# Spectral and attention layers on one core: three row blocks of the second spectral layer prepared inside the first attention loop

## The chip, the cores and the metric

The kernel runs on one core of a Trainium2 chip. A core has five engines that work side by side, each through its own instructions in order: TensorE (PE; its weight loads are listed as PEld), VectorE (DVE), ScalarE (ACT), GpSimd (POOL) and SyncE (SP, which here only starts transfers). They share an on-chip memory, and PE writes its results to a second one, PSUM, of eight banks. The metric is the time of one execution on the device in microseconds; lower is better.

## The reference

Two pairs of layers work on x, a bf16 array of 2048 rows by 512. A spectral layer normalises each row, takes a real 2-D Fourier transform, multiplies with fixed complex weights, transforms back and adds the result to x. An attention layer normalises each row, makes queries of 32 heads of 16 numbers, and one set of keys and values for all heads, and adds the projected result to x.

```
def _A_ref(x, w_r, w_i):
    X = rfft2(x.astype(float32), axes=(-2, -1))
    X = X * (w_r + 1j * w_i)
    return irfft2(X, s=(S, D), axes=(-2, -1)).astype(bfloat16)

def _B_ref(x, wq, wk, wv, wo):
    q = (x @ wq).reshape(B, S, 32, 16).transpose(0, 2, 1, 3)
    k, v = x @ wk, x @ wv
    scores = einsum("bhqd,bkd->bhqk", q, k) * 16 ** -0.5
    p = softmax(scores, axis=-1)
    o = einsum("bhqk,bkd->bhqd", p, v)
    return o.transpose(0, 2, 1, 3).reshape(B, S, 512) @ wo

x = x + _A_ref(_layernorm(x), A_w_r, A_w_i)
x = x + _B_ref(_layernorm(x), B_wq, B_wk, B_wv, B_wo)
x = x + _A_ref(_layernorm(x), A_w_r, A_w_i)
x = x + _B_ref(_layernorm(x), B_wq, B_wk, B_wv, B_wo)
```

## The kernel before, in words

Everything stays on the chip between the layers. The 2048 rows lie as `x_sb[p, r, t, :]`: 128 partitions p, four row groups r (each 512 rows), four interleaved parts t. A row block t is the four groups r at one t. The outer loop (`pair`) runs twice: a spectral layer, then an attention layer.

**Spectral layer.** For each row block t, `scaled` normalises the four groups (`Norm.apply`: one ACT or DVE instruction of 128x512 for each group, from the row statistics that `Norm.stats` made on DVE and that `Norm.root` and `Norm.scales` turned into a factor and an offset). `butterfly` (L155) then takes sums and differences of the four groups and of the halves of their columns: six DVE `tensor_tensor` operations, which write Z, block t. Z lies in the buffer `xz`, which holds the transposed rows `xT` for the queries and keys during attention. `odd_sums` and `even_sums` are PE matmuls with Z as the stationary operand and a table of cosines and sines as the moving one: a length-2048 transform cut to a quarter by the butterfly. A group of odd sums adds over all four row blocks in one PSUM bank, so its last matmuls need block 3. `middle` then transforms over the width, multiplies with the weights and transforms back over the width; `blocks` transforms back over the rows with the tables IO and IE, adds to x, and makes `xT`, the keys and the values of the attention layer.

The front differs between the two spectral layers. `front_first` waits for loads. `front_next` (L863), the second layer's, follows the first attention loop: block 3 of x (and only it) is still without its attention result, since the last query block's last head group has just ended. It scales blocks 0 to 2, and between their butterflies and sums it finishes that last projection: `last_scale` divides by the softmax sums and transposes back (DVE), `last_project` multiplies with wo (PE, three of four pieces ahead of `last_scale`, the fourth behind it), `last_residual` adds to x (DVE). Then statistics, root and scaling of block 3, its butterfly, its sums.

**Attention loop** (`Attention.run`). It has 32 groups, eight for each query block (512 queries), a group being four heads. A group has 64 tiles of 128 keys by 512 queries for one head. The loop goes in some 579 steps, about 18 in a group; a step's work on each engine is put in an order by hand, and `chain` (L422) fixes that order for PE, ACT, DVE and Pool. In a step
- PE makes scores for two or three tiles (`act_step`) and ACT takes their exponential in one instruction (L609);
- 19 tiles of a group get no exponential from ACT. For them DVE turns scores into a bf16 bit pattern (`dv_pass`, L643, `t_new`); three shifted copies of that pattern ("images") are added up instead of an exact exponential. DVE makes two of the images for a whole phase at once (`image_step`, L658, `s_new`, at the first and the fourth of a phase's six steps) and Pool the third tile by tile (L662, `pool_new`);
- PE multiplies exponentials and images with the values (`pv_step`, L622), two or more steps later.

`pace` (L535) makes a Pool instruction wait for the newest s_new, so Pool works in bursts between two of them. Other work comes at fixed steps: `evict` takes a group's result (DVE transpose, L550), `normalise` divides it (Pool, L565, `od_new`), `turned_back` transposes (DVE, L571), `piece` makes the next group's queries or projects a row group of the query block before (PE), and `residual` (L587) adds it to x on DVE. Some steps later, as `STAT` says, `finish` calls `row_done`: in the first loop the row's statistics (DVE) and, when a block's four rows are done, four small Pool instructions for its factors and offsets; in the second loop the store of the row to HBM, from SP or Pool in turn. `later` and `later_pool` queue such work on DVE and Pool.

Behind the second loop the last projection is made with four PSUM banks (pool `psE`), DVE adds, and the last four rows are stored.

Outside the loops a scheduler may move an instruction ahead, but within each manual schedule the order of PE, ACT and DVE is the program's. PSUM and work memory are handed from one stage's pools to the next tile by tile.

## Time and profile before

| what | us |
|---|---|
| median of 3 runs | 1586.08 (1585.1 to 1587.77) |
| the profiled execution's own time | 1586.75 |
| its span on the core | 1584.6 |
| busy ACT / DVE / PE / POOL | 1445.6 / 1418.6 / 1363.6 / 795.8 |
| L609, exponentials | 1315.7 in 1158 |
| L643, t_new on DVE | 792.3 in 1204 |
| L662, pool_new on Pool | 747.1 in 1204 |
| L658, s_new on DVE | 385.9 in 380 |

The span is what the profiler saw on the core; the time has some 2 us more around it. Busy time is what an engine's instructions took. In lists of groups, instructions of one source line, engine and shape stand together. In a timeline a row is a start, a duration, the engine, the line, what is written and read, how many equal instructions follow each other, and in brackets how long the engine had been idle and what released it. In the chain, the work that ended last is followed back, at each step to what released it. The granted clock is the share of TensorE's full clock.

### The profile page before, as it was taken

Reading aid. Unit: us, or ns where it says so; the run is one execution under the profiler, and the core shown is the slowest. Engines: PE = TensorE matmul, PEld = TensorE weight load, DVE = VectorE, ACT = ScalarE, POOL = GpSimd, SP = SyncE. Lnnn points to the kernel's source line nnn. Section 1 sums busy time; section 2 is a strip of 40 time slices with the busy share of each in tenths; the row PEclk is TensorE's granted clock in tenths of the full one; section 3 lists DMA queues with packets and bytes.
Section 4 is the critical chain, followed back from the end, with each engine's and each line's share of the span. In section 5 each row is a group of like instructions: output and inputs, shape, how many; then the busy total and the mean of one; then the engine's idle time right before and its main releaser. Section 6 shows DMA issues by size and latency. Waiting matters only on the chain.

```text
span 1584.6 us, 33064 instructions
## 1 busy us (share of the span) xinstructions
PE 1363.6 (86%) x13244; PEld 430.9 (27%) x13244; DVE 1418.6 (90%) x2260; ACT 1445.6 (91%) x1358; POOL 795.8 (50%) x1310
## 2 busy tenths in 40 slices
PE   5978888899889988898879688888998899889987
PEld 2432222222222222222234322222222222222222
DVE  6587999999999999999866889999999999999996
ACT  6658999999999999999944599999999999999997
POOL 1003655565656565656600045555556656665555
PEclk9997999999999999999989789999999999999999
DMA  7000000000000000000000000000000000000000
GB/s 269 14 1 1 2 1 1 1 1 2 1 2 1 2 1 1 1 2 1 2 0 1 1 1 2 1 2 1 5 5 5 5 5 5 5 5 5 5 1 21
DMA packets 12910, 15.37 MB, mean 10 GB/s; under 512 B 5716, under 2 KB 10452, under 8 KB 12628
## 3 DMA queue, kind: packets, MB, share of 16 engines
q1 hardware_dynamic: 12372, 12.22, 2.3%
q8 instruction: 103, 1.69, 0.5%
q0 software_dynamic: 384, 1.05, 0.2%
q14 instruction: 51, 0.42, 0.1%
HBM read 11.17 MB, written 2.10 MB: 8 GB/s over the span
## 4 chain that ended last, share of the span: by engine, by line
DVE 36%; ACT 31%; PE 15%; issue 14%; POOL 4%; DMA 0%; DVEq 0%; POOLq 0%; ACTq 0%
ACT e L609 30%; DVE t_new L643 16%; DVE s_new L658 9%; POOL pool_new L662 4%; PE pv_new L622 3%; PE sc L531 3%; PE new L199 3%; DVE st L103 2%; PE new L286 2%; DVE o L550 1%; DVE qt L345 1%; DVE ot_new L571 1%; PE dv L531 1%; PE new L235 1%; PE new L234 1%
## 5 line engine op out<-in xcount | busy, mean ns | idle before, releaser
L609 ACT ACTIVATE e<-sc 128x1536 bf16<-128x1536 f32 (+1 forms) x1158 | 1315.7, 1293 | 21.9 <-PE dv L531 19.3
L662 POOL TENSOR_SCALAR pool_new<-t_new 128x512 int16<-128x512 int16 x1204 | 747.1, 643 | 746.7 <-DVE s_new L658 566.4
L643 DVE TENSOR_SCALAR t_new<-dv 128x512 uint16<-128x512 f32 x1204 | 792.3, 678 | 77.1 <-PE dv L531 62.3
L622 PE MATMUL pv_new<-e,vaug 128*32 128x512 bf16 x2892 | 593.3, 388 | 0.0
L531 PE MATMUL sc<-qt,KT 32*128 32x512 bf16 x2892 | 457.8, 386 | 117.0 <-ACT e L609 109.9
L531 PE MATMUL dv<-qt,KT 32*128 32x512 bf16 x1204 | 455.1, 387 | 21.5 <-DVE t_new L643 19.7
L622 PE MATMUL pv_new<-s_new,vaug 128*32 128x512 bf16 x2408 | 421.1, 385 | 5.7 <-DVE s_new L658 5.7
L658 DVE TENSOR_SCALAR s_new<-t_new 128x3584 int16<-128x3584 int16 (+1 forms) x380 | 385.9, 1016 | 0.1
L622 PE MATMUL pv_new<-pool_new,vaug 128*32 128x512 bf16 x1204 | 298.7, 386 | 21.1 <-POOL pool_new L662 21.1
L531 PEld LDWEIGHTS <-KT 32*128 32x128 bf16 x4096 | 155.9, 91 | 561.6 <-issue 555.2
L622 PEld LDWEIGHTS <-vaug 128*32 128x32 bf16 x7708 | 153.8, 94 | 397.6 <-issue 365.4
L622 PE MATMUL pv_new<-t_new,vaug 128*32 128x512 bf16 x1204 | 232.0, 386 | 0.1
L340 PE MATMUL ps<-xz,wq_sb 128*128 128x512 bf16 x256 | 67.2, 385 | 0.6 <-ACT KT L386 0.6
L199 PE MATMUL new<-tab_F,xz 128*128 128x512 bf16 x192 | 52.7, 433 | 9.9 <-DVE xz L164 9.9
L550 DVE STREAM_TRANSPOSE o<-pv_new 128x512 f32<-128x512 f32 x64 | 45.3, 707 | 13.6 <-PE pv_new L622 13.6
L103 DVE BATCH_NORM_STATS2 st<-x_sb 128x6 f32<-128x512 bf16 x64 | 43.0, 671 | 3.8 <-DMA x_sb<-in_A_x_dram 3.5
L345 DVE CAST qt<-ps 128x512 bf16<-128x512 f32 x64 | 43.6, 682 | 1.2 <-PE ps L340 1.2
L565 POOL TENSOR_TENSOR od_new<-o,den 128x256 bf16<-128x256 f32 x62 | 38.5, 620 | 0.0
L107 ACT ACTIVATE ln_rstd<-ln_mv,ln_eps 128x4 f32<-128x4 f32 x13 | 3.9, 297 | 29.6 <-DVE ln_mv L104 29.4
L340 PEld LDWEIGHTS <-wq_sb 128*128 128x128 bf16 x256 | 21.9, 97 | 31.1 <-issue 16.3
L199 PEld LDWEIGHTS <-xz 128*128 128x128 bf16 x192 | 20.2, 109 | 36.5 <-DVE xz L164 11.2
L318 PE MATMUL new<-G_new,tab_IE 128*128 128x512 bf16 x128 | 28.9, 379 | 0.0
(92 smaller groups left out, 614.0 us busy)
## 6 DMA issues: line engine op xcount, KB each, us to landing
tab_F<-const_F SPq DMA_DIRECT2D x4, 640.0 KB, 11.9
x_sb<-in_A_x_dram SPq DMA_DIRECT2D x4, 512.0 KB, 4.6
rt<-in_A_w_r_dram SPq DMA_DIRECT2D x1, 1028.0 KB, 7.5
rt<-in_A_w_i_dram SPq DMA_DIRECT2D x1, 1028.0 KB, 11.7
tab_IE<-const_IE SPq DMA_DIRECT2D x1, 1024.0 KB
out_dram<-x_sb SPq DMA_DIRECT2D x8, 128.0 KB, 1.7
out_dram<-x_sb POOLq DMA_DIRECT2D x8, 128.0 KB, 2.2
tab_I<-const_I SPq DMA_DIRECT2D x1, 768.0 KB, 6.0
```

Source lines behind the costliest of these rows:

```text
L103: self.nc.vector.bn_stats(st, x_ap)
L199: self.mm(ps, lhsT=z, rhs=tab, start=(t == 0 and (i == 0 or mms[i - 1][1] != 0)), stop=(t == T - 1 and i == len(mms) - 1))
L340: self.nc.tensor.matmul(ps, lhsT=self.aw["wq"][:, c, hg, :], rhs=self.xT[:, c, 4 * qb:4 * qb + 4, :].rearrange("d k p -> d (k p)"), start= ...
L345: self.nc.vector.tensor_copy(out=qt, in_=ps)
L531: nc.tensor.matmul(dst, lhsT=KT[hs, kc * P:(kc + 1) * P], rhs=QT[g][hs, :], start=True, stop=True)
L550: nc.vector.transpose(out=o.rearrange("p c j -> p (c j)"), in_=ps)
L565: return engine.tensor_tensor(out=turned_od[g // 2][:, :, half], in0=o[:, :, 0:DH], in1=den.unsqueeze(2).broadcast_to([P, 16, DH]), op=ALU ...
L609: nc.scalar.activation(out=e[:, 0:na, :], in_=sc[:, 0:na, :], func=ACT.Exp, scale=SCALE)
L622: nc.tensor.matmul(pv[g][32 * h:32 * h + 32, :], lhsT=vaug[:, max(j, 0), kc, :], rhs=rhs, start=(first_pv[(g, h)] == u), stop=(last_pv[(g, ...
L643: nc.vector.tensor_scalar(out=tb[(g, b)][:, i, :], in0=dv, scalar1=T_MUL, scalar2=T_ADD, op0=ALU.mult, op1=ALU.add)
L658: image[0] = nc.vector.tensor_scalar(out=s_new[:, lo:nt, :], in0=src[:, lo:nt, :], scalar1=PH_OFF[i], scalar2=None, op0=ALU.add)
L662: pace(nc.gpsimd.tensor_scalar(out=sb[(g, b, 3)][:, i, :], in0=src[:, i, :], scalar1=1.0, scalar2=PH_OFF[3], op0=ALU.mult, op1=ALU.add))
```

## The change

Row blocks 0 to 2 of the second spectral layer are scaled and go through their butterfly inside the first attention loop. When the fourth row of a block has its statistics, `finish` queues, behind the four small Pool instructions, four scalings on Pool (every second step), and then the butterfly: for blocks 0 and 1 on Pool, cut into 20 pieces of 256 elements a partition, one every second step; for block 2 on DVE in six whole operations at fixed steps of the last group. The results go to Z, whose blocks now lie in `xz` as `(i t)` and not `(t i)`: block t of Z fills exactly the place of query block t's transposed rows, which are free by then. For block 2's four rows the steps at which their statistics are taken (in the second loop: their stores) move ahead by up to two groups.

`front_next` is left with the last projection, block 3 and the sums: all sums of blocks 0 to 2 follow each other. The last projection no longer ends with an add on DVE: PE multiplies the old rows with an identity matrix into the same PSUM bank ahead of the projection, and ACT (behind the second loop ACT and DVE in turn) copies the sum to x. Its four banks come from the stage's own pool. Block 3 is scaled by one ACT and three DVE instructions.

For the space of the new tiles the tables IO and IE are no longer kept all the time: they lie in each spectral layer's work pool, and are loaded twice.

```diff
+LAST_B = (13, 14, 16, 16, 17, 18)
...
+def butterfly_pieces(nc, engine, norm, small, x_sb, Z, t, width):
+    tiles = {}
+    tt = engine.tensor_tensor
+    def scaled(r):
+        if r == 0:
+            X_new = small.tile([P, 4, 512], BF, tag="bx", bufs=1)
+            s_new = small.tile([P, 2, 512], BF, tag="bs", bufs=1)
+            e_new = small.tile([P, 4, 512], BF, tag="be", bufs=1)
+            tiles.update(X=X_new, s=s_new, e=e_new)
+        norm.apply(nc.gpsimd, x_sb[:, r, t, :], tiles["X"][:, r, :], r, t)
+    def first(op, a, b):
+        X, dst = tiles["X"], tiles["s"] if op is ALU.add else tiles["e"][:, 2:4, :]
+        return tt(out=dst[:, :, a:b], in0=X[:, 0:2, a:b], in1=X[:, 2:4, a:b], op=op)
+    def second(op, a, b):
+        sm = tiles["s"]
+        return tt(out=tiles["e"][:, 0 if op is ALU.add else 1, a:b], in0=sm[:, 0, a:b], in1=sm[:, 1, a:b], op=op)
+    def third(op, a, b):
+        e, lo = tiles["e"], 0 if op is ALU.add else 256
+        return tt(out=Z[:, t, :, lo + a:lo + b], in0=e[:, :, a:b], in1=e[:, :, 256 + a:256 + b], op=op)
+    rows = [lambda r=r: scaled(r) for r in range(R)]
+    rest = []
+    for fn, n, w in ((first, 512, width // 2), (second, 512, width), (third, 256, width // 4)):
+        for op in (ALU.add, ALU.subtract):
+            rest += [lambda fn=fn, op=op, a=a, w=w, n=n: fn(op, a, min(a + w, n)) for a in range(0, n, w)]
+    return rows, rest
...
-            g, i = divmod(k, 4)
-            g = min(HG * (g + 1) + 5 + i, NG - 1)
-            later(max(2, s0[g] + STAT - now[0]), lambda: finish(k))
-
-        def finish(k):
-            for i, fn in enumerate(row_done(k % 4, k // 4) or ()):
+            if t == NQB - 2:
+                n = s0[NG - 3 + r // 2] + (4, 14)[r % 2]
+            else:
+                n = s0[HG * (t + 1) + 5 + r] + STAT
+            later(max(2, n - now[0]), lambda: finish(r, t))
+
+        def finish(r, t):
+            roots = row_done(r, t) or ()
+            for i, fn in enumerate(roots):
                 later_pool(1 + i, fn)
+            if roots:
+                own = t == NQB - 2
+                rows, rest = butterfly_pieces(nc, nc.vector if own else nc.gpsimd, self.norm, small, x_sb, self.Z, t, 2048 if own else 256)
+                for i, fn in enumerate(rows):
+                    later_pool(len(roots) + 2 + 2 * i, lambda fn=fn: fn())
+                for i, fn in enumerate(rest):
+                    if own:
+                        later(s0[NG - 1] + LAST_B[i] - now[0], fn)
+                    else:
+                        later_pool(len(roots) + 10 + 2 * i, lambda fn=fn: pace(fn()))
...
+        def last_project(i, ps, end):
+            ot = otc[NQB - 1]
             if not end:
-                ps_new = psum.tile([P, 512], F32, tag="mm", bufs=bufs)
-                last_ps[i] = ps_new
+                nc.tensor.matmul(ps, lhsT=tabs["EYE"][:, 0, :], rhs=x_sb[:, i, T - 1, :], start=True, stop=False)
             for c in (3,) if end else range(3):
-                nc.tensor.matmul(last_ps[i], lhsT=otc[NQB - 1][:, c, i * P:(i + 1) * P], rhs=wo_sb[:, c, :], start=(c == 0), stop=(c == 3))
-
-        def last_residual(i):
-            nc.vector.tensor_tensor(out=x_sb[:, i, T - 1, :], in0=last_ps.pop(i), in1=x_sb[:, i, T - 1, :], op=ALU.add)
+                nc.tensor.matmul(ps, lhsT=ot[:, c, i * P:(i + 1) * P], rhs=wo_sb[:, c, :], start=False, stop=(c == 3))
...
     def front_next(work, sp, psum, last):
...
-        X0 = scaled(work, 0, (nc.scalar, nc.vector) * 2)
-        X1 = scaled(work, 1, (nc.scalar,) * 4)
-        X2 = scaled(work, 2, (nc.scalar,) * 4)
         nc.scalar.activation(out=norm.nb[:, t3, 0:1], in_=norm.eps, func=ACT.Sqrt)
...
+        two = sp.big()
+        ps = [two[:, 0, :], two[:, 1, :], sp.bank(), sp.bank()]
+        for i in range(R):
+            last_project(i, ps[i], False)
         last_scale()
+        for i in range(R):
+            last_project(i, ps[i], True)
+        for i in range(R):
+            nc.scalar.copy(out=x_sb[:, i, t3, :], in_=ps[i])
             norm.stats(x_sb[:, i, t3, :], i, t3)
         norm.root(t3)
         norm.scales(t3)
+        X3 = scaled(work, t3, (nc.scalar, nc.vector, nc.vector, nc.vector))
+        for _ in butterfly(nc, work, X3, Z[:, t3, :, :]):
             pass
         for dc in range(4):
+            sp.odd_sums(dc, range(t3))
         for dc in range(3):
             sp.odd_sums(dc, (t3,))
...
-                for name in ("F2", "I1", "IO", "IE", "KAB", "QAND"):
+                for name in ("F2", "I1", "KAB", "QAND"):
                     table(name)
+            for name in ("IO", "IE"):
+                t_new = work.tile(list(ht[name].shape), BF, tag=name)
+                if pair == 0:
+                    inverse[name] = nc.inline_tensor(ht[name], name=f"const_{name}").ap()
+                nc.sync.dma_start(out=t_new, in_=inverse[name])
+                tabs[name] = t_new
...
+            for i in range(R):
+                last_project(i, ps[i], True)
+            for i in range(R):
+                (nc.vector.tensor_copy, nc.scalar.copy)[i % 2](out=x_sb[:, i, T - 1, :], in_=ps[i])
                 row_done(i, T - 1)
```

## The prediction

> **What bounds the kernel now.** I read the profile in this order: stages, chain, then what the two attention loops wait for. First the table of stages (stretch, length, busy time of each engine, granted clock, DMA):
> ```profile
> 125.35:791.60 666.25, 586.75 (x6068) 169.72 (x6065) 625.17 (x967) 657.90 (x579) 395.39 (x645) 0.99 0.01 1
> 791.60:823.82 32.22, 22.69 (x81) 8.87 (x79) 22.23 (x46) 13.04 (x19) 0.00 (x0) 0.79 0.00 0
> 823.82:908.28 84.46, 71.11 (x447) 34.92 (x446) 60.54 (x115) 44.84 (x71) 0.00 (x0) 0.92 0.00 1
> 908.28:1575.10 666.82, 585.22 (x6068) 168.56 (x6065) 618.20 (x943) 657.80 (x579) 393.66 (x639) 0.99 0.01 4
> ```
> The columns of busy time are PE, PEld, DVE, ACT, POOL. The loops are 84% of the span, and ACT is busy 657.9 of 666.3 us in each: 579 exponentials, 1.151 us a step. The first loop carries ten rows' statistics on DVE and the Pool's roots, the second none; they differ by 0.6 us, so work that only fills DVE's idle 6% costs nothing. The second stretch is the second spectral layer's front, the change's place: no engine is full, and PE's clock is 0.79. Its chain:
> ```profile
> 790.58 1.63 PE pv_new L622 x18
> ...
> 796.42 5.30 PE new L199 x12
> 801.73 1.78 PE ps_new L718 x7
> ...
> 809.29 0.18 DVE ln_mv L104
> ...
> 810.90 12.92 PE new L199 x48
> 823.82 0.22 PE new L234
> ```
> PE ends its attention work at 792.2, waits for DVE's first butterfly until 796.4, runs twelve sums at 0.42 us each (half clock), projects, and waits again from 806 to 810.9 for the last rows' statistics. From 792.2 to 823.8 are 31.6 us; PE's 76 matmuls in them are 16.4 us at the full-clock pitch of 0.215 us (the L234 row). The other 15.2 us are waits and slow clock.
>
> The loop's weak spot is Pool against DVE. One case, each engine's line from its own timeline:
> ```profile
> 224.16 4.81 POOL L662 TENSOR_SCALAR pool_new<-t_new 128x512 int16<-128x512 int16 x7 [1.80 <-DVE s_new L658]
> 225.80 0.96 DVE L658 TENSOR_SCALAR s_new<-t_new 128x3072 int16<-128x3072 int16 x1
> 227.28 0.38 PE L622 MATMUL pv_new<-pool_new,vaug 128*32 128x512 bf16 x1 [0.98 <-POOL pool_new L662]
> 228.11 1.45 ACT L609 ACTIVATE e<-sc 128x1536 bf16<-128x1536 f32 x1 [0.63 <-PE dv L531]
> ```
> Seven images at their pitch of 0.59 are 4.1 us; here 4.8, since one met an s_new. PE waited 0.98 for that image, and ACT stood idle 0.63. The other way round DVE pays: an s_new that meets a Pool operation takes 1.48 instead of 1.08. Over the first loop:
> ```profile
> 780.84 1.48 DVE L658 TENSOR_SCALAR s_new<-t_new 128x3584 int16<-128x3584 int16 x1
> ```
> ```profile
> PE pv_new L622 <- POOL pool_new L662: 10.9, 13, 1.0
> ACT e L609 <- PE dv L531: 7.5, 12, 1.0
> ```
> So 13 late images in 32 groups, 0.63 us of ACT's time each.
>
> **Part 1, the front.** Gone from it are 13 of ACT's 14 scalings (0.80 each; DVE's two become three), three butterflies of 3.3 us on DVE and its four residual adds (0.67). Their sum means nothing: what counts is PE's waits. In the changed program's order PE, straight after its last attention matmul, does four rows of one identity and three projection matmuls, then the four last ones, the 48 sums of blocks 0 to 2, and the 12 of block 3: 80 matmuls. At 0.216 us they are 17.3 us. Must PE wait in between? The last operands follow DVE's transpose, reciprocal, multiply and transpose, 2.3 us in the last projection's rows (1575.77 to 1578.05), so they are there at 794.5; PE gets to them at 792.2 + 16 x 0.216 = 795.7. Then ACT's four copies (0.58 for a cast of this size, L386) feed four statistics at a pitch of 0.80: root at 800.1; scalings from 800.9 (0.74 behind a root, as at 872.73), done by 802.0; first half of the butterfly 2.7 us later, 804.8. PE needs it at 796.5 + 48 x 0.216 = 806.9. So block 3's whole chain is hidden under 48 sums with 2.1 us to spare; without that cover it would cost 8.3 us. The square root's table load (1.28 us, as in the row below) now stands behind ACT's copies; free from 798.3 to 800.1, or 1.3 of the 2.1 us. Sum: 31.6 - 17.3 = **14.3 us gained**. Late next is PE itself. Bounds: none more below; should the clock drop to half for a while, five microseconds at 0.42 cost 2.5, two such stretches 5.
>
> **Part 2, the Pool in the first loop.** Blocks 0 and 1 each bring Pool 4 scalings and 20 adds of 256 elements, one every second step, from group 16 and group 24 on. No row of the trace has a bf16 add on Pool. Nearest is the same operation, size and engine:
> ```profile
> L565 POOL TENSOR_TENSOR od_new<-o,den x62: 617/620/622, 158.7 to 1562.4; 128x256 bf16<-128x256 f32 x62
> ```
> From below, the 4-element multiply takes 0.198 (L120), and images cost 0.82 ns an element over that: 0.41. I take 0.62, in a queue 0.59. Half a phase (three steps) is 3.45 us: an s_new of 0.98, 3.2 images (1.9 us), and 0.4 us free before the next s_new. The added 1.5 operations are 0.88 us, 0.48 too much, so nearly every half-phase collides, 31 times in 2 x 47 steps. Most images bear it: an operation late by 0.6 matters only for those that PE takes at once, now 13 in 32 groups. The 94 steps are 5.2 groups; I let every one of them have such an image, one or two additions (0.6 to 1.2 us) late: 3.1 to 6.2, **4.5 us lost**. From below 0: in the 0.41 case the overhang is 0.2 and DVE's own idle, 0.21 us per half-phase, takes it. From above 17: 31 x 0.48 and block 2's four scalings (2.4) all paid. Nothing is behind these adds on Pool but the images and od_new, whose transpose on DVE has no wait now.
>
> The Trainium skill, page "SBUF — State Buffer", section "Who interferes with whom", says that the pair of ports shared by the two engines is an exclusive lock, held for a whole instruction. The trace's 4.81 and 1.48 agree in kind. Its strict form is the third rival, worked out there from rows.
>
> **Part 3, DVE in the loop's tail.** Block 2's butterfly (six operations, 3.3 us) stands beside the last two s_new, where two statistics (1.6 us) leave, and in a gap where DVE now idles 5.27 us before L550. Pool loses its roots there (1.6 us) and may be blocked by the six: 0 to +2, **0.5** taken, since the gap is nearly as long as the work. The statistics moved two groups forward add 0.86 us to a group that has 1.3 idle: nothing.
>
> **Part 4, the start of loop one.** The dummy square root was held in the front by the scalings before it. It is now first there, needs only old data, and in the built program stands in the first layer, between the dummy exponential and a copy:
> ```profile
> 116.38 1.28 ACT L986 ACT_TABLE_LOAD   x1
> 118.46 1.01 ACT L376 COPY xz<-ps 128x1024 bf16<-128x1024 bf16 x1 [0.58 <-PE ps L370]
> 119.32 0.69 DVE L374 COPY xz<-ps 128x1024 bf16<-128x1024 bf16 x1 [1.02 <-PE ps L370]
> 120.07 1.89 PE L384 MATMUL ps<-xz,wka 128*128 128x512 bf16 x4 [0.79 <-DVE xz L374]
> ```
> ACT is free at 117.9; a load and the root take it to 119.4, the copy ends 120.4 instead of 119.5, and PE, which had waited for DVE until 120.0, starts **0.4** late. The exponential's table is loaded again (1.28) while DVE scales the keys (122.6 to 124.6): hidden, else 1.3.
>
> **Part 5, the rest.** Tables IO and IE are loaded twice; SP issues the second load at about 792, 512 KB landed in 6.8 us before and a 1 MB one in 7.5 to 11.7, and they are first read 36 us after the sums end: free. At the end four identity matmuls (0.9) precede and two adds go to ACT: row 2, whose store ends the chain, is ready at 1580.8 instead of 1580.5: **0.3**, at most -0.3.
>
> Sum: -14.3 + 4.5 + 0.5 + 0.4 + 0.3 = -8.6. The profiled execution took 1586.75 us (span 1584.6), 0.67 over the median 1586.08; 1586.75 - 8.6 - 0.67 gives **1577.5**.
>
> **Rivals.** (1) The adds are cheap or never catch an urgent image: loop cost 0, tail 0, 1586.1 - 14.3 + 0.7 = 1572.5. For it: loop one carries 10 us more DVE work than loop two for nothing. Against: the 0.98 wait above. (2) PE drops to half clock in the front, as it did at 796.4 after 4.2 us of idling: +4, 1581.5. Against: the new order leaves no gap. (3) Pool sets the pace in 31 half-phases. If s_new and Pool only alternate, one lasts 0.98 + 4.84 x 0.59 = 3.84 (3.17 images, 1.5 additions, a sixth of an od_new) instead of 3.45: 12.1 us, 1585.1. If the whole overhang and block 2 are paid, 17 us: 1590.0, slower. It turns the sign from 13.1 us of loop cost on, that is 0.42 a half-phase. For it: ACT, DVE and PE are 99, 94 and 88% busy, so there is little to take a delay. Against: in the trace a burst's first image is ready some 4 us before PE reads it, and PE waited 13 times only although Pool met an s_new in about every group.
>
> **How the numbers follow.** Forecast (1574.5 to 1580.5) 0.46, rival 1 0.17, rival 2 0.15, rival 3 alternating 0.09, rival 3 in full 0.13. A difference under 0.2% (3.2 us) is no change: faster 0.78, same 0.09, slower 0.13. The range from 1571.5 (rival 1 and a bit) to 1585.5 (alternating) leaves the full rival 3 and about 0.04 of others out.
>
> **What would show it.** Stretch from the last pv_new to the first L269 (old L234): 17.3 us, clock near 1.0, else step 1 is wrong. Loop one longer than loop two by 4 to 6 us, all of it in groups 16 to 19 and 24 to 27; PE's wait for pool_new up from 10.9 to about 16. Pool's adds 0.62 each. A loop one longer by 13 us or more makes the forecast wrong.

## The result, and the profile after

The changed kernel takes 1592.03 us (median of 5 runs, 1591.04 to 1593.59), the kernel before beside it 1585.1 us: a ratio of 1.0042, with a 95% interval of 1.0027 to 1.0056. It is slower by 6.9 us between the medians; the forecast was 8.6 us faster.

First the stages of the changed kernel (stretch, its length, busy time of PE, PEld, DVE, ACT, POOL with the number of instructions, granted clock, DMA). The first row is loop one from its first to its last exponential, then groups 17 to 19 of it, its last group, the front, and loop two:
```profile
125.51:809.05 683.54, 592.15 (x6013) 169.47 (x6056) 640.32 (x973) 659.93 (x578) 451.38 (x697) 0.98 0.01 1
478.25:545.58 67.33, 58.67 (x570) 16.27 (x579) 63.30 (x92) 62.44 (x56) 62.33 (x88) 0.97 0.01 2
781.14:809.05 27.91, 21.12 (x195) 5.48 (x198) 23.87 (x30) 23.16 (x21) 23.96 (x31) 0.88 0.01 1
810.63:828.03 17.40, 17.30 (x79) 7.84 (x82) 10.86 (x25) 5.62 (x9) 0.00 (x0) 1.00 0.23 77
912.32:1579.05 666.73, 583.07 (x6017) 167.86 (x6059) 618.75 (x943) 657.51 (x578) 395.58 (x639) 0.99 0.01 4
```
and the same three groups and the last group of the kernel before:
```profile
478.58:540.46 61.88, 56.34 (x576) 16.16 (x579) 59.26 (x92) 61.67 (x55) 38.63 (x64) 1.00 0.01 2
...
768.30:790.93 22.63, 18.37 (x199) 5.69 (x201) 18.11 (x28) 22.63 (x21) 16.09 (x25) 1.00 0.01 2
```
The front is what was forecast: 17.40 us at full clock. Loop two is 0.5 us longer than before (666.7 against 666.2 us between its first and last exponential), within what executions differ. Loop one is 18.0 us longer than before (683.5 against 665.6, the latter from the first to the last exponential in the same way). In groups 17 to 19 the Pool went from 38.6 to 62.3 us busy for 24 more operations, whose own work is 4 x 0.77 + 20 x 0.67 = 16.5; the other 7 us it stood inside an operation, blocked. DVE's busy time rose by 4.0 us with the same 92 instructions.

Laid out over the loop (loss against before, from the start of the exponentials; one execution each):
```
groups                        0-16   17-20  21-24  25-28  29-end   loop one
changed kernel                -0.5    5.5    0.0    6.9     6.1      18.0
```
So the parts of the difference between the two profiled executions (spans 1589.6 and 1584.6, +5.0) are: start of loop one +0.2, loop one +18.0, the front from the last exponential of one loop to the first of the next -14.1, loop two +0.5, end +0.4.

Two rows of the waits of the changed kernel (us in total, times, longest) answer to the two of before, over both loops; there they were 21.1 us and 19.3 us:
```profile
PE pv_new L670 <- POOL pool_new L710: 26.3, 25, 4.4
ACT e L657 <- PE dv L566: 26.0, 33, 2.2
```
They grew by 5.2 and 6.7 us, and the 4.4 is new. In groups 17 to 20 and 25 to 28 together, PE's waits for images grew by 2.1 us and its waits for DVE's t_new and s_new by 5.3 us, so the larger part of the lateness there comes by way of DVE. How the loss arises is seen in the timelines. At the start of block 0 (start, duration, engine, line, operation, in brackets the idle time before it and what ended it):
```profile
487.71 0.77 POOL L130 TENSOR_SCALAR X_new<-x_sb,ln_rstd,ln_nb 128x512 bf16<-128x512 bf16 x1
487.81 2.20 DVE L706 TENSOR_SCALAR s_new<-t_new 128x3584 int16<-128x3584 int16 x1
488.45 0.62 POOL L710 TENSOR_SCALAR pool_new<-t_new 128x512 int16<-128x512 int16 x1
489.94 0.67 DVE L691 TENSOR_SCALAR t_new<-dv 128x512 uint16<-128x512 f32 x1
...
490.66 0.37 PE L566 MATMUL dv<-qt,KT 32*128 32x512 bf16 x1 [1.36 <-DVE t_new L691]
...
492.48 1.02 ACT L657 ACTIVATE e<-sc 128x1024 bf16<-128x1024 f32 x1 [1.37 <-PE dv L566]
```
A scaling on the Pool begins 0.10 us ahead of an s_new. s_new takes 2.20 instead of 1.08: it waits for the scaling (until 488.48), and also for the image that stood behind the scaling in the Pool's queue (until 489.07), and then runs 0.94. DVE's next t_new is late, so PE's bank for the next score is, so the exponential: ACT stands idle 1.37. The forecast had let one s_new pay at most 0.4 (1.48 against 1.08). The Trainium skill, page "SBUF — State Buffer", section "Who interferes with whom", calls the shared pair of ports an exclusive lock; the 2.20 agrees, and shows that two Pool operations can come first.

And in the loop's last group:
```profile
797.03 0.77 POOL L130 TENSOR_SCALAR X_new<-x_sb,ln_rstd,ln_nb 128x512 bf16<-128x512 bf16 x1
797.21 1.40 DVE L706 TENSOR_SCALAR s_new<-t_new 128x3072 int16<-128x3072 int16 x1
797.77 9.33 POOL L710 TENSOR_SCALAR pool_new<-t_new 128x512 int16<-128x512 int16 x10
798.54 1.09 DVE L185 TENSOR_TENSOR s_new<-X_new 128x1024 bf16<-128x1024 bf16 x1
799.54 1.09 DVE L185 TENSOR_TENSOR e_new<-X_new 128x1024 bf16<-128x1024 bf16 x1
800.56 1.37 DVE L706 TENSOR_SCALAR s_new<-t_new 128x3072 int16<-128x3072 int16 x1
...
802.45 0.58 PE L670 MATMUL pv_new<-pool_new,vaug 128*32 128x512 bf16 x1 [4.41 <-POOL pool_new L710]
...
803.72 2.53 ACT L657 ACTIVATE e<-sc 128x1536 bf16<-128x1536 f32 x2 [4.19 <-PE sc L566]
```
The last scaling of block 2 goes ahead of ten images, the ten take 0.93 each where 0.59 is their pitch, the additions on DVE take 1.09 where 0.69 is normal, and PE waits 4.41 us for an image. The Trainium skill, in the same page and section, says that a DVE instruction with two inputs in SBUF contends with a GpSimd one that reads SBUF; 0.69 against 1.09 agrees.

### The profile page after: what moved, and what is told of

It is laid out like the page before. It is cut to its first block, busy times and chain, and to the rows that moved or that the text cites. A ratio compares the mean times of both kernels' runs of the same rounds, so it can differ in the third digit from the quotient of the medians.

```text
span 1589.6 us, 33014 instructions
## 1 busy us (share of the span) xinstructions
PE 1363.3 (86%) x13145; PEld 430.3 (27%) x13252; DVE 1421.6 (89%) x2243; ACT 1445.0 (91%) x1353; POOL 853.7 (54%) x1362
## 3 DMA queue, kind: packets, MB, share of 16 engines
q8 instruction: 103, 1.69, 0.5%
## 4 chain that ended last, share of the span: by engine, by line
DVE 37%; ACT 28%; PE 16%; issue 13%; POOL 6%; DMA 0%; DVEq 0%; POOLq 0%; ACTq 0%
ACT e L657 27%; DVE t_new L691 17%; DVE s_new L706 10%; POOL pool_new L710 6%; PE pv_new L670 4%; PE sc L566 3%; PE new L233 2%; DVE st L104 2%; PE new L320 2%; DVE o L585 1%; DVE qt L380 1%; DVE ot_new L606 1%; PE dv L566 1%; PE new L269 1%; PE new L268 1%
## 5 line engine op out<-in xcount | busy, mean ns | idle before, releaser
L710 POOL TENSOR_SCALAR pool_new<-t_new 128x512 int16<-128x512 int16 x1204 | 763.5, 658 | 693.0 <-DVE s_new L706 611.0
L566 PE MATMUL dv<-qt,KT 32*128 32x512 bf16 x1204 | 456.1, 388 | 25.5 <-DVE t_new L691 23.9
L706 DVE TENSOR_SCALAR s_new<-t_new 128x3584 int16<-128x3584 int16 (+1 forms) x380 | 394.5, 1038 | 0.1
L670 PE MATMUL pv_new<-t_new,vaug 128*32 128x512 bf16 x1204 | 235.5, 391 | 0.0
L375 PE MATMUL ps<-xz,wq_sb 128*128 128x512 bf16 x194 | 63.6, 385 | 4.8 <-ACT KT L421 0.6
L585 DVE STREAM_TRANSPOSE o<-pv_new 128x512 f32<-128x512 f32 x64 | 45.2, 706 | 14.3 <-PE pv_new L670 14.3
L233 PE MATMUL new<-tab_F,xz 128*128 128x512 bf16 x187 | 47.0, 401 | 1.2 <-DVE xz L165 1.0
L600 POOL TENSOR_TENSOR od_new<-o,den 128x256 bf16<-128x256 f32 x62 | 38.6, 622 | 0.0
L352 PE MATMUL new<-G_new,t_new 128*128 128x512 bf16 x126 | 28.8, 379 | 0.1
L320 PE MATMUL new<-tab_I,SD_new 128*128 128x512 bf16 x124 | 27.7, 379 | 0.2
L321 ACT CAST G_new<-new 128x1024 bf16<-128x1024 f32 x16 | 16.2, 1012 | 12.2 <-PE new L320 12.2
```

Of the source, the lines that this page charges most:

```text
L233: self.mm(ps, lhsT=z, rhs=tab, start=(t == 0 and (i == 0 or mms[i - 1][1] != 0)), stop=(t == T - 1 and i == len(mms) - 1))
L320: self.mm(ps[:, i, :], lhsT=self.SD[blk][:, fc, sd, ks], rhs=I1[:, tab, fc, :], start=(fc == 0 and n == 0), stop=(fc == 1 and n == 1))
L375: self.nc.tensor.matmul(ps, lhsT=self.aw["wq"][:, c, hg, :], rhs=self.xT[:, c, 4 * qb:4 * qb + 4, :].rearrange("d k p -> d (k p)"), start= ...
L566: nc.tensor.matmul(dst, lhsT=KT[hs, kc * P:(kc + 1) * P], rhs=QT[g][hs, :], start=True, stop=True)
L585: nc.vector.transpose(out=o.rearrange("p c j -> p (c j)"), in_=ps)
L670: nc.tensor.matmul(pv[g][32 * h:32 * h + 32, :], lhsT=vaug[:, max(j, 0), kc, :], rhs=rhs, start=(first_pv[(g, h)] == u), stop=(last_pv[(g, ...
```

## The experiments

My theory at first was this: the loss of blocks 0 and 1 comes from Pool operations that meet s_new, one by one; that of the last group from DVE's butterfly of block 2. The rivals: the Pool is simply overfull (one addition every second step), or the loop has no room for added work on any engine. All loop figures below are from one profiled execution each, summed up in a table at the end; the times are medians with their runs.

**The last group: which part of block 2?** Two kernels take block 2 apart. In the first its butterfly is moved to the front, and the Pool still scales it in the loop; in the second the scaling is in the front too (on ACT). In both, the sums of block 2 come behind those of blocks 0 and 1.
```
-                    later(s0[NG - 1] + LAST_B[i] - now[0], fn)      (kernel 1: butterfly of block 2)
+        for fn in front: fn()                                       (behind last_scale in front_next)

-            if roots:
+            if roots and t in (0, 1):                               (kernel 2: nothing of block 2)
+        X2 = scaled(work, 2, (nc.scalar,) * 4)
+        for _ in butterfly(nc, work, X2, Z[:, 2, :, :]): pass       (behind last_scale)
```


> Blocks 0 and 1 as in the change; block 2 is still scaled by the Pool in the loop, but DVE's butterfly of block 2 (six two-input operations) stands in the front, behind the last scaling of the heads. The tail of loop one lost 6.0 us. Theory A (those six operations hold what DVE and the Pool share, so the last group's images are late): the tail's loss falls to about 1, the front costs at most 1 more; 1592.0 - 5 + 0.5 = 1587.5, images of the last group back at about 0.6 us each, PE's 4.41 us wait for pool_new gone. Theory B (the Pool is late there for its four scalings and roots alone): the tail keeps its loss, 1591 to 1592.5.

> As the run before, but block 2 is also scaled in the front, by ACT, so that nothing of block 2 is in the loop; blocks 0 and 1 as in the change. Theory A: as the run before within 1 us, 1586 to 1587.5, since the scalings on the Pool cost the tail little. Theory B: only here the tail's 6 us come back: 1586 to 1587 here against 1591 to 1592.5 there. In both the loop keeps the 12.3 us lost in groups 17 to 20 and 25 to 28.

Measured: 1595.13 (4 runs, 1591.1 to 1596.7; ratio 1.0059, interval 1.0042 to 1.0076) for the first, 1588.27 (10 runs; ratio 1.0016, interval 1.0006 to 1.0025) for the second. From group 29 to the end the first still lost 5.2 us of the 6.1, the second 1.6. Theory A fell: the butterfly was worth 0.9 us, the scalings with what they delay 3.6. Both figures include a slower clock in the last group, of which more below the table. The profiled execution of the first was 5.3 us longer than the changed kernel's, but little over 1 us of that is in loop one; the rest is ahead of it, in loop two and at the end. In loop one, block 0 lost 8.6 us instead of 5.5 with the same instructions in those groups, and block 1 lost 5.3 instead of 6.9.

**No preparation in the loop.** All of it is in the front, with the change's order of the projection; then the same with the statistics of rows 2 back at their steps of before.
```
-            if roots:
+            if roots and t in ():

-            if t == NQB - 2:
-                n = s0[NG - 3 + r // 2] + (4, 14)[r % 2]
-            else:
-                n = s0[HG * (t + 1) + 5 + r] + STAT
+            n = s0[min(HG * (t + 1) + 5 + r, NG - 1)] + STAT        (second kernel only)
```


> Nothing of the second spectral layer is prepared in the loop: all sixteen scalings (ACT, two on DVE) and four butterflies (DVE) stand in the front, with the change's new order of the projection (old rows through the identity, no residual add on DVE). If the loop's 18 us come from that preparation alone, loop one is as long as loop two again and the whole loss is gone; the front then waits for DVE's butterflies and I estimate it 4 to 6 us longer than in the changed kernel: 1592.0 - 18 + 5 = 1579, between 1575 and 1581, faster than both. If part of the 18 us comes from anything else that the change moved in the loop (statistics two groups earlier, the dummy root), that part stays: above 1582.

> The kernel that prepares nothing in the loop (1580.7, loop one 668.2), with the statistics of rows 2 back at the steps that the kernel before gave them. Its tail lost 2.0 us against before, all of it in the last three groups: with no statistic between them the last two s_new stand back to back, and the Pool's ten images start at 7.2 us before the last exponential instead of being under way. If that is the cause, loop one is 666 again and the time 1578.5 to 1579. If the tail's loss has another cause, 1580.7 stays.

Measured: 1580.73 (ratio 0.9970, 0.9958 to 0.9981) and 1577.04 (0.9940, 0.9921 to 0.9959). Loop one is 2.6 us longer than before in the first and 0.0 us in the second: nothing else that the change does in the loop costs anything. The 2.6 us are the statistics that the change moved ahead by up to two groups, and about half of it is paid at each end of the move. The first kernel has two statistics each in groups 29 and 30 (at steps 4 and 14) where the second has one, and each of these groups takes 0.6 us longer in the first. The last group, which the statistics left, takes 1.3 us longer. Its end in the first kernel:
```profile
785.47 2.25 DVE L706 TENSOR_SCALAR s_new<-t_new 128x3072 int16<-128x3072 int16 x2
785.50 6.19 POOL L710 TENSOR_SCALAR pool_new<-t_new 128x512 int16<-128x512 int16 x8
788.24 0.38 PE L670 MATMUL pv_new<-pool_new,vaug 128*32 128x512 bf16 x1 [1.30 <-POOL pool_new L710]
```
and of the second:
```profile
785.35 0.69 DVE L104 BATCH_NORM_STATS2 st<-x_sb 128x6 f32<-128x512 bf16 x1
785.88 3.66 POOL L707 TENSOR_SCALAR pool_new<-t_new 128x512 int16<-128x512 int16 x5
...
786.55 0.38 PE L667 MATMUL pv_new<-pool_new,vaug 128*32 128x512 bf16 x1 [0.62 <-POOL pool_new L707]
...
786.96 0.93 DVE L703 TENSOR_SCALAR s_new<-t_new 128x3072 int16<-128x3072 int16 x1
```
In the first the last two s_new stand back to back (2.25) and hold the Pool's images back; in the second a statistic stands between them, in which the Pool works, and PE waits 0.62 instead of 1.30. That work on DVE was a gap for the Pool.

These two kernels also say what the preparation is worth in the front. From the last exponential of loop one to the first of loop two the second takes 107.2 us, against 117.3 before and 103.3 in the changed kernel: 10.2 of the 14.1 us gained there need nothing prepared in the loop, and only some 4 us are left for the preparation to earn.

**The Pool's additions: density or place?** From the second kernel above, with the 20 additions of each block at other steps: every fourth, every sixth, or four in the middle of each group.
```
-   later_pool(len(roots) + 10 + 2 * i, lambda fn=fn: pace(fn()))
+   later_pool(len(roots) + 10 + 4 * i, lambda fn=fn: pace(fn()))                           (gap 4)
+   later_pool(len(roots) + 10 + 6 * i, lambda fn=fn: pace(fn()))                           (gap 6)
+   later_pool(s0[HG * t + 18 + i // 4] + 5 + 2 * (i % 4) - now[0], lambda fn=fn: pace(fn()))   (mid)
```


> As the run before, with the 20 additions of blocks 0 and 1 on every fourth step instead of every second. The additions and scalings cost 12.3 us in the two stretches, of which I read 2.3 a block as the scalings' and 3.2 to 4.5 as the additions'. Theory of the overfull queue (half a phase holds 3.2 images and one and a half additions, more than its 3.45 us): at half the density there is room, the additions' 6.5 to 8 us shrink to 0 to 2, and the time is 1579 to 1582. Theory of the price per meeting (each addition that meets a subtraction delays DVE or an image that PE takes at once, however far apart they stand): the same sum spread over twice the steps, 1585 to 1587.

> The kernel with one addition every fourth step on the Pool (1584.9; groups 18 to 20 and 26 to 28 lost 0.26, 0.45, 0.26 and 0.27, 0.06, 0.27, then 1.5 and 1.7 in groups 21 and 29), with one edit: the 20 additions go to steps 5, 7, 9 and 11 of five groups, so none is queued between step 12 and step 4 of the next group, when the last images of a group are made. Half of ACT's idle time in the changed kernel stands at steps 4 and 16 to 17 (0.91, 0.40; 1.04 and 0.91, 0.39; 4.19 in the last group), where PE waits for a group's last image. If the price of an addition is its place before those images: four additions a group cost 0 to 0.2 a group, loop one 672 to 673, with the scalings' 2 us a block left, 1581. If the price is the density (four a group as against four and a half): as before, 1584 to 1585.

> The Pool's additions once more, one every sixth step (gaps 2 and 4: a loss of 1.4 to 1.7 and of 0.06 to 0.45 for each full group without statistics, 1588.3 and 1584.9). Theory of density on the Pool: three additions a group cost 0 to 0.15 in groups 18 to 20 and 26 to 28, and little more in groups 21 to 23: loop one 672 to 673, 1581. Theory of DVE's slack: the price is paid wherever DVE's idle time is already used, so groups 21 to 23 and 29 to 31, which have statistics and now have additions too, lose 0.5 to 1.5 each, and the time stays at 1583 to 1586.

Measured: 1584.88 (10 runs, 1582.3 to 1589.6; ratio 0.9999, 0.9986 to 1.0012), 1589.5 (1.0024, 1.0013 to 1.0036) and 1590.01 (1.0034, 1.0022 to 1.0046), against 1588.27 at gap 2. Gap 4 took a quarter of loop one's loss off (15.0 to 10.9); gap 6, thinner still, gave it all back (15.5). Two things go against each other here. At gap 2 all additions are done by the end of group 19 and of group 27, in stretches where the Pool is hardly ever idle (62.3 of 67.3 us busy in the changed kernel); thinned to gap 4 and 6, groups 17 to 20 and 25 to 28 together lose 5.8 and 6.9 us instead of 12.4. But thinner additions reach into groups 21 to 23 and 29 to 31, and there the loss grows, from 2.6 to 5.0 and 9.1. So density alone is not it: at gap 6 the Pool is busy 43.4 of the 66.6 us of groups 21 to 23,
```profile
564.17:630.78 66.61, 56.16 (x574) 15.32 (x567) 61.36 (x95) 62.29 (x54) 43.42 (x69) 0.95 0.01 2
```
and these three groups are still 4.8 us longer than before (61.79). The mid placement fell as I had put it, too, since it lost nearly as much as gaps 2 and 6. But where it lost is telling. Group 21, mid placement, where the images of the group's second phase end:
```profile
580.65 0.67 POOL L193 TENSOR_TENSOR xz<-e_new 128x256 bf16<-128x256 bf16 x1
581.29 2.48 POOL L710 TENSOR_SCALAR pool_new<-t_new 128x512 int16<-128x512 int16 x3
581.72 1.00 DVE L706 TENSOR_SCALAR s_new<-t_new 128x3072 int16<-128x3072 int16 x1
583.74 0.66 POOL L193 TENSOR_TENSOR xz<-e_new 128x256 bf16<-128x256 bf16 x1
583.82 0.38 PE L670 MATMUL pv_new<-pool_new,vaug 128*32 128x512 bf16 x1 [1.62 <-POOL pool_new L710]
...
584.65 2.48 ACT L657 ACTIVATE e<-sc 128x1536 bf16<-128x1536 f32 x2 [1.13 <-PE dv L566]
```
and the same place at gap 6:
```profile
580.04 0.67 POOL L193 TENSOR_TENSOR xz<-e_new 128x256 bf16<-128x256 bf16 x1
580.68 3.65 POOL L710 TENSOR_SCALAR pool_new<-t_new 128x512 int16<-128x512 int16 x5
580.82 1.30 DVE L706 TENSOR_SCALAR s_new<-t_new 128x3072 int16<-128x3072 int16 x1
582.64 0.38 PE L670 MATMUL pv_new<-pool_new,vaug 128*32 128x512 bf16 x1 [1.34 <-POOL pool_new L710]
```
This is the urgent burst of seven images, the one for which PE waited 0.98 us in the kernel before. One addition (0.67) ahead of its last images, and the wait is 1.34 to 1.62. My "middle of the group" still put its third addition there: issued at step 9, run two steps later. The place in the group is not enough either. In group 18 of the same execution the Pool does the same in the same order (an addition of 0.67 at 516.99, then three images in 2.48), and PE does not wait for them, as it does not wait there in groups 17 to 20 and 25 to 28 of the kernel before. Those groups have a projection piece on PE at step 13 and, apart from the changed work, no statistic on DVE; groups 21 to 24 and 29 to 31 have the statistic and no projection. The kernel before also waits there, 0.98 us, in groups 2, 4, 6 and 8, which have neither, so the projection, which PE does before it takes the images, is the likelier reason; that was not tested. Gap 4 is the cheapest of the three because it thins the first stretches and puts only the last additions of each block ahead of an urgent burst (1.62 and 1.64 us of waiting, in groups 21 and 29); gap 6 does so in six groups.

**The scalings.** Once a step later on the Pool, once on DVE, both from the second kernel (gap 2).
```
-   later_pool(len(roots) + 2 + 2 * i, lambda fn=fn: fn())
+   later_pool(len(roots) + 3 + 2 * i, lambda fn=fn: fn())          (a step later)

-   norm.apply(nc.gpsimd, ...)                                       (on DVE)
+   norm.apply(nc.vector, ...)
-   later_pool(len(roots) + 2 + 2 * i, ...)   and   later_pool(len(roots) + 10 + 2 * i, ...)
+   later(len(roots) + 8 + 2 * i, ...)        and   later_pool(len(roots) + 18 + 2 * i, ...)
```


> The kernel with block 2 in the front (1588.3; group 17 lost 2.3, group 25 1.9), with its eight scalings on the Pool each one step later. In the traces the loss of that group is one meeting: a scaling begins 0.10 us ahead of an s_new, an image stands behind it, and s_new takes 2.20. One step is 1.15 us, so this meeting can't be the same. If the price hangs on such single meetings, group 17's loss changes by a microsecond or more either way, 0 to 1.2 or above 3. If four scalings of 0.77 cost what they cost wherever they stand, it stays between 1.9 and 2.5 and the time at 1588.

> The kernel with block 2 in the front (1588.3, loop one 680.6), with one edit: the eight scalings of blocks 0 and 1 on DVE (0.39 us each) instead of on the Pool, 12 steps behind the roots; the additions stay on the Pool, one every second step. The lock theory (a Pool operation in progress holds back the s_new that arrives, and with it DVE's next tile, PE's scores and ACT; one such chain is 2.20 us of s_new at 488.51 where 0.95 is normal): the 2.1 to 2.3 us lost within a group of each block's scalings go, loop one 676 to 677, 1584. The theory that the loop is full and any added operation costs its own time: 8 x 0.39 = 3.1 us replace them, 1587.

Measured: 1587.38 (1.0013, 1.0003 to 1.0022) and 1590.28 (1.0027, 1.0018 to 1.0036): no gain from either, loop one 15.1 and 15.3 us over before. A step later, the meeting of the 2.20 is gone: the six s_new of group 17 sum to 6.06 us (7.80 in the kernel compared with). Group 17 lost 2.0 us instead of 2.3 all the same (and group 25 3.0 instead of 1.9, with a drop of the clock of which more below the table), now at its end and on the other engine:
```profile
494.88 1.54 POOL L130 TENSOR_SCALAR X_new<-x_sb,ln_rstd,ln_nb 128x512 bf16<-128x512 bf16 x1
494.91 0.95 DVE L706 TENSOR_SCALAR s_new<-t_new 128x3072 int16<-128x3072 int16 x1
496.39 0.61 POOL L710 TENSOR_SCALAR pool_new<-t_new 128x512 int16<-128x512 int16 x1
496.97 0.66 POOL L185 TENSOR_TENSOR s_new<-X_new 128x256 bf16<-128x256 bf16 x1
497.61 1.77 POOL L710 TENSOR_SCALAR pool_new<-t_new 128x512 int16<-128x512 int16 x3
498.85 0.38 PE L670 MATMUL pv_new<-pool_new,vaug 128*32 128x512 bf16 x1 [1.64 <-POOL pool_new L710]
...
499.86 1.02 ACT L657 ACTIVATE e<-sc 128x1024 bf16<-128x1024 f32 x1 [1.80 <-PE dv L566]
```
Now s_new goes first, the scaling is blocked (1.54 instead of 0.77), an addition follows it, and PE waits 1.64 for the image behind both. With the scalings on DVE, four of them within seven steps cost 1.0 us in group 17, and the additions, eight steps later, cost nearly as much as scalings and additions together had (some 5 us a block): an addition at 549.33 ahead of the images that end group 19 made PE wait 1.03 and ACT 1.34 there, the latter with PE at half clock. That the meetings can be counted one by one, 2.1 us a block for the scalings, fell with these two runs. In both kernels the backlog of the Pool was paid somewhere, by DVE or by PE.

**The same work on DVE.** Blocks 0 and 1 are prepared in whole tiles on DVE (5.2 us a block), at steps that were chosen; block 2 in the front, statistics as before. Three placements: one or two operations a group in eight groups; all in the four groups without statistics at steps 1 and 14; the same four groups at step 14 alone, with the last operation of each block in the front.
```
-   rows, rest = butterfly_pieces(nc, nc.vector if own else nc.gpsimd, ..., 2048 if own else 256)
+   rows, rest = butterfly_pieces(nc, nc.vector, ..., 2048)
+   for (g, k), fn in zip(PREP[t], rows + rest): later(s0[g] + k - now[0], fn)
+   PREP[0] = (17,14) (17,14) (18,14) (18,14) (19,14) (20,14) (21,1) (22,1) (23,1) (24,1)      (first)
+             (17,14) (17,14) (17,14) (18,1) (18,14) (19,1) (19,14) (20,1) (20,14) (20,14)     (second)
+             (17,14) x3, (18,14) x2, (19,14) x2, (20,14) x2, then the front                    (third)
```


> No operation of the second spectral layer is left on the Pool: the scalings of blocks 0 and 1 and their butterflies are on DVE, in whole tiles (5.2 us a block: four of 0.39, four of 0.69, two of 0.42), each put at a step of its own: the statistics' steps of groups 17 to 20 and 25 to 28, and one step early in groups 21 to 24 and 29 to 31. Block 2 in the front, statistics at their times of before. Lock theory: DVE's idle time, 1.3 us a group beside the statistics, takes one or two of these a group; loop one 666 to 669, and with the front as in the changed kernel 1573 to 1576, the fastest so far. Theory that the loop is full: 10.4 us of DVE's time are paid, loop one 676, 1583.

> As the kernel with the preparation on DVE (loop one 669.6, 1576.4), whose 4.0 us of loss stood only in groups 21 to 24 (2.3) and 30 to 31 (1.4), where a statistic of 0.84 or the group's end already filled DVE's idle time, and was zero in groups 17 to 20 and 25 to 28. Here all ten operations of a block (5.2 us) are in four groups without statistics, 17 to 20 and 25 to 28, at steps 1 and 14. If DVE's idle time of some 1.3 us a group is all that counts: the load is 1.17, 1.08, 1.11 and 1.80 a group, of which only the last is too much, by 0.5: loop one 666.5 to 667, 1573.0 to 1574. If the place in the group matters (step 1 always costs the operation's length): 0.39 + 0.42 + 0.42 a block and 0.5, 3.5 in all: loop one 669, 1576.

> The preparation on DVE once more (1575.2, loop one 669.1, 3.5 us above before: 0.42, 0.51 and 0.37 for the operations at step 1 of groups 18 to 20 and 0.68 for the second one at the statistics' step of group 20; the same for block 1). Now all of it stands at the statistics' steps of groups 17 to 20 and 25 to 28 (1.17, 1.08, 1.11 and 1.11 us there, of which 1.17 cost nothing in the run before), and the last operation of each block, 0.69, in the front behind the last scaling of the heads. If such a step takes 1.17 free of charge: loop one 665.6 to 666; the front has some 0.8 us to spare before block 3's sums and gets 1.4 more: +0.6; 1572 to 1573. If 1.08 to 1.17 were free in group 17 alone, by its own gap: 1574 to 1575.5.

Measured: 1576.4 (4 runs, 1575.6 to 1577.7; ratio 0.9938, 0.9917 to 0.9958), 1575.21 (5 runs, 1575.1 to 1578.5; 0.9937, 0.9924 to 0.9949) and 1575.73 (6 runs, 1574.1 to 1578.5; 0.9939, 0.9926 to 0.9951). All three beat the kernel before and the changed kernel, and can't be told from each other. "The loop is full" fell: in the first kernel six operations a block at step 14 cost 0.0 us. So did "idle time is all that counts": in the second the operations at step 1 of groups 18 to 20 cost 0.42, 0.51 and 0.37 us, which is their own length, though these groups have no statistics. An operation on DVE costs its length at step 1; at step 14, 0.7 to 0.8 us are free (in group 17 even 1.17). In the third, where 1.1 us stand at step 14 of three more groups of each block, 0.1 to 0.5 us of it is paid each time: loop one 2.0 us over before, between the two expectations. The kernel with everything in the front (1577.04, interval 0.9921 to 0.9959) beats both as well, and by these intervals can't be told from the three: preparing blocks 0 and 1 in the loop, even on DVE, brought nothing that the runs show. Groups 17 to 19 of the second:
```profile
478.34:541.14 62.80, 56.83 (x570) 15.98 (x579) 61.68 (x99) 62.00 (x55) 38.87 (x64) 1.00 0.01 2
```
DVE is busy 98% of that stretch, with seven instructions more, and it is 0.9 us longer than before; in the changed kernel DVE had none of this work and the stretch was 5.5 us longer.

The losses of loop one against before, us, one execution each:
```
groups                             0-16   17-20  21-24  25-28  29-end   loop one
changed kernel                     -0.5    5.5    0.0    6.9     6.1      18.0
block 2's butterfly in the front    0.1    8.6    0.0    5.3     5.2      19.2
block 2 in the front, gap 2         0.1    5.4    1.0    7.0     1.6      15.0
  gap 4                             0.1    2.9    1.5    2.9     3.5      10.9
  gap 6                            -0.6    3.7    4.8    3.2     4.3      15.5
  additions in the middle           0.2    3.3    3.7    2.9     4.1      14.2
  scalings a step later             0.0    6.9    0.0    6.3     1.8      15.1
  scalings on DVE                   1.1    6.4    0.0    6.2     1.6      15.3
all in the front                    0.2    0.3    0.0    0.0     2.2       2.6
  statistics as before              0.1    0.3    0.0    0.0    -0.4       0.0
on DVE, first placement             0.1    0.1    2.3    0.0     1.5       4.0
  second                            0.0    1.3    0.7    1.3     0.3       3.5
  third                             0.2    0.6    0.5    0.6     0.1       2.0
```
The groups are cut here at every 18th exponential, two ahead of a group's first one. The 0.7 and 0.5 in the last two rows under groups 21 to 24 are therefore what step 14 of group 20 cost, and the columns behind them shift in the same way.

**What the clock adds.** From 160 us on, the granted clock is 1.00 throughout loop one in the kernel before, in the last kernel with everything in the front and in the three with the work on DVE. In every kernel with additions on the Pool it drops to 0.50, for 3.4 us at a time (6.8 in some last groups), behind some of PE's waits: in the changed kernel at 491.2, 661.8, 699.4 and 801.8 us. (The first kernel with everything in the front has one, in its last group.) Group 27 of the changed kernel and of the one with block 2's butterfly in the front have the same operations and the same wait of PE for an image (1.03 us), one with such a drop and one without:
```profile
696.48:720.05 23.57, 20.75 (x195) 5.41 (x193) 20.84 (x31) 20.97 (x19) 20.47 (x30) 0.93 0.01 2
700.93:723.24 22.31, 19.47 (x197) 5.38 (x193) 20.66 (x31) 20.79 (x19) 21.32 (x30) 1.00 0.01 2
```
PE's work takes 1.3 us longer in the first, and so does the group. In group 19 it is the other way round: 22.3 us at clock 1.00 in the changed kernel, 23.9 at 0.93 in the other, which has a drop in group 18 as well. In the kernel with the scalings on DVE, group 14, where nothing was changed, lost 0.95 us with a drop behind the same wait as before. So a drop costs some 1.0 to 1.5 us, and two of them are most of what makes 8.6 out of 5.5 for the same instructions. The last group has 6.8 us of half clock in the changed kernel, 10.2 with block 2's butterfly in the front and none with all of block 2 there, so the 0.9 and 3.6 us above contain what it cost. Why one wait is followed by a drop and another isn't, no run shows: most waits of 0.98 us, all of those in the kernel before among them, had none.

## Why the prediction was wrong

**Part 1, the front: right.** 17.4 us as forecast (17.3), granted clock 1.00; from the last exponential of loop one to the first of loop two 103.3 us instead of 117.3, 14.1 gained for a forecast of 14.3. PE did not stop for block 3: with block 2's butterfly, and in the third placement on DVE two more operations, on DVE ahead of it, that stretch stayed at 102.9 to 103.3 us (104.3 at gap 6, where it began at half clock). The rival with the half clock didn't occur in the front; half clock came in the loop, where the prediction had not put it. And 10.2 of the 14.1 us come without any preparation in the loop.

**Part 2, the Pool in the first loop: this failed, by path and by size.** It said 4.5 us for blocks 0 and 1; they cost 12.4. The path that was priced is an image that PE takes at once, made late by one or two additions. It exists: 1.03 us twice in the changed kernel, 1.34 to 1.64 in others. But PE's waits for images grew by only 2.1 us in these groups. Its waits for DVE's t_new and s_new, as in the first timeline above, grew by 5.3 us, and for that path the sum had no term. The sign that was set, PE's wait for images in loop one up from 10.9 to about 16 us, came true (16.1), but by luck: 4.4 of it are the one wait in the last group, for which it was not meant. The term mis-sized is "I let every one of them have such an image, one or two additions (0.6 to 1.2 us) late": over the 5.2 groups the loss was 2.4 us a group. An addition took 0.67 and not 0.62, a scaling 0.77; both were small errors. The larger ones: a scaling has no pacing, and an s_new that meets it waits for two Pool operations, 2.20 instead of the 1.48 on which the estimate rested; there are several urgent places in a group (the burst of seven and the group's last images), where I had counted one; and the clock drops behind some of the waits, at 1.0 to 1.5 us each where two executions can be compared.

The upper bound of 17 was not far, and the time came within 2 us of rival 3 in full (1590.0). Rival 3's alternating case, with the Pool's throughput as the pace, had 12.1 us for the blocks. The runs don't exclude it for the dense stretches, where the Pool was busy 62.3 of 67.3 us (7 of them blocked) and where half the density halved the loss. It isn't the whole: with additions a third as dense and the Pool 65% busy, groups 21 to 23 lost 4.8 us. How the 12.4 divide between a full Pool, single meetings and the clock stays open. The opposite, rival 1, "loop one carries 10 us more DVE work than loop two for nothing", was true of DVE at the step where the statistics stand and not elsewhere, and was read over to the Pool, for which no row spoke.

**Part 3, the loop's tail: this failed outright.** Forecast +0.5 (0 to +2), measured +6.1. "The statistics moved two groups forward add 0.86 us to a group that has 1.3 idle: nothing" was wrong by 2.2 to 2.6 us. Half was the place they went to: a second statistic, at step 4, cost groups 29 and 30 0.6 us each, idle time of 1.3 or not. The other half was the place they left, where they had kept two s_new apart. Block 2's scalings on the Pool were not priced in this part at all (only in Part 2's upper bound); together with what they delay they cost some 3.6 us, the difference between the two kernels with block 2's butterfly in the front. The butterfly on DVE, which alone had been weighed, cost about 0.9. PE's wait of 4.41 us and 6.8 us of half clock behind it are what the last group shows in their place.

**Part 4, the start: small, and so it was.** Loop one began 0.2 us later, not 0.4. Its start on the clock of the trace moves by more than that between kernels without the hoisted root (0.3 earlier to 1.1 later than before). But counted from the table load of the dummy exponential, the first exponential starts after 9.22 us in the two kernels that have the hoisted root and after 8.95 to 8.97 in the kernel before and the eleven others, so the root costs 0.25 us.

**Part 5, the end: right.** From the last exponential to the end 10.5 us instead of 10.15.

With the forecast's own other terms, 12.4 in place of 4.5 and 6.1 in place of 0.5 make 1577.5 + 7.9 + 5.6 = 1591.0; measured 1592.0. The mark set beforehand, "a loop one longer by 13 us or more makes the forecast wrong", was met with 18.0.

## What to carry to other kernels

An engine with idle time isn't an engine with room: ask which of its results are taken at once, what an added operation in its in-order queue stands in front of, and which other engine it holds back. The Pool was 59% busy here and 24 small operations cost 5 to 7 us a block; the same work on DVE, 94% busy, cost 2 to 4 us for both blocks together, and six of the ten operations, at the right step, nothing. In this kernel, work that two engines contend over was cheapest on the engine that the critical step already waits for. Before a small operation is moved out of a tight place, look at who used the gap that it made and at the place where it goes. And before work is moved at all, measure the change without the move: here the new order of the front alone gave a time that no placement clearly beat.

## What was not expected of the hardware

A DVE instruction that contends with the Pool can wait for two Pool instructions in a row, when the second is ready as the first ends (2.20 us of an s_new of 1.08, in five of these kernels). The reverse costs the Pool as much: a scaling of 0.77 took 1.54 to 1.69, an addition of 0.67 took 1.44. Which of the two pays can't be foretold from who begins first: a scaling that began 0.10 us ahead of an s_new held it (2.20), one that began 0.03 us ahead was held by it (1.54).

A wait of PE can cost twice. Behind some waits of about 1 us or more the granted clock was 0.50 for 3.4 us, and a group with the same operations and the same wait took 1.3 us longer with that drop than without.
